# A second step, a product with one, in GpSimd's scaling of attention weights and its minimum

## The chip, the core and the metric

The kernel runs on one core of a Trainium2 chip. A core has five engines that follow their own instruction streams and wait for each other by semaphores: TensorE (PE, with its weight loads PEld), VectorE (DVE), ScalarE (ACT), GpSimd (POOL) and SyncE (SP, which here only issues DMAs). The metric is the device time of one execution in microseconds (us), lower is better.

## The reference

Three layers run one after the other, all in float32: attention with a memory, a gated layer, and a second layer with a squared, cut-off activation.

```python
# attention, B=4, H=8, S=576, D=64
scores = where(causal, -1e9, q @ k.T / 8)
a = exp(scores - scores.max(-1));  a /= a.sum(-1) + 1e-9
local = a @ v
phi = lambda x: where(x > 0, x, exp(x) - 1) + 1
mem = (phi(q) @ M_prev) / ((phi(q) * z_prev).sum(-1) + 1e-6)
x = sigmoid(beta) * mem + (1 - sigmoid(beta)) * local     # -> 2304 x 512
# layer 1 (512 -> 1536 -> 512)
x = (silu(x @ w_gate) * (x @ w_val)) @ w_out
# layer 2 (512 -> 2048 -> 512), g(h) is 0 below -1, h above 1, (h+1)^2/4 between
return g(x @ w_in) @ w_out2
```

The weights `a` are divided by their row sums before the product with v; the kernel does this as a multiplication by one reciprocal per row, and folds the factor 1 - sigmoid(beta) into it.

## The kernel before

The program has two stages, each laid out by its own planner (`Plan`). The first holds the attention and a part of layer 1, the second the rest. This case lives in the first stage, which on the trace fills about the first 260 us.

**The work of the attention.** `Attention.pair(b, n)` describes one pair of heads of one batch entry; there are 16 pairs. For a pair the program loads q, k and v, transposes k and q on TensorE (L607, L618), forms the scores on TensorE (L725 and, for the last 64 rows of both heads together, L759), adds the mask and takes the row extreme on VectorE (L739, L766), and applies exp on ScalarE with the row sums as a by-product (L746, L777). Two small VectorE instructions (L802, L807) then turn the sums into reciprocals `r`, one number for each row. Next comes the scaling of this case (function `scale`, L812 to L820): each tile `a` of attention weights is multiplied in place by its column of `r`. After that TensorE transposes the tile (L830, L852, L869), ScalarE or VectorE copies the transposed tile out of PSUM (L513), and TensorE multiplies with v (L894, L902).

Each pair has nine tiles to scale: four tiles of 128, 256, 384 and 512 columns for each of two heads, since the mask leaves only the lower triangle, and one of 576 columns for the last rows. So the kernel has 144 scalings. A string of digits (`CHOICE`) says for each of them whether GpSimd or VectorE does it: 77 are on GpSimd, 67 on VectorE.

The memory branch works on the same engines: the minimum of q with zero (`f_min`, L635), exp (L638), `p` (L642), its product with z (L647, L651), two folding additions (L658), and the multiplication by the norm (L668). Of the 16 minima one is on GpSimd and 15 on VectorE.

**The early part of layer 1.** TensorE also gets matmuls of layer 1 in this stage (L1308), on the rows of x that are complete.

**What sets the order.** `Plan.order` runs through all tasks by priorities from a fixed list (`RANK`), with a duration for each, and writes each engine's instructions down in the order that results. The engines then follow this order strictly: an instruction that waits holds up all that stand behind it on its engine. The durations that the planner used are formulas in the code. For a scaling on GpSimd it is `c_pool(cols)`, to which the plan adds 43 ns for each task of this engine; for the minimum it is a number written out:

```python
def c_pool(n):                       # L369, ns
    return 0.835 * n + 285
over={"PE": 1, "ACT": 2, "DVE": 9, "POOL": 43},          # L1250
both = [("POOL", c_pool(cols), lambda: f(nc.gpsimd), False),
t = choose("min", [("POOL", 1580, lambda: f_min(nc.gpsimd), False),
```

The change leaves every one of these numbers as it is.

Of the kernel before, what the change touches and what calls it, by code (L numbers as in the profile page):

```python
# [9 lines left out]
F32 = mybir.dt.float32  # L10
# [4 lines left out]
ALU = mybir.AluOpType  # L15
# [4 lines left out]
P = 128  # L20
# [124 lines left out]
class Inst:  # L145


    def __init__(self, tag):
        self.tag, self.left, self.held, self.slot = tag, 0, False, None
# [207 lines left out]
def c_dve(n):  # L357
    return 0.52 * n + 68
# [10 lines left out]
def c_pool(n):  # L369
    return 0.835 * n + 285  # L370
# [23 lines left out]
class Attention:  # L394
# [3 lines left out]
    def __init__(self, ctx, tc, plan, q, k, v, M_prev, z_prev, beta, cst, xs):  # L398
        self.tc, self.nc, self.plan = tc, tc.nc, plan
        nc = tc.nc  # L400
        self.q, self.k, self.v, self.M, self.z, self.beta = q, k, v, M_prev, z_prev, beta
        self.ident = cst["ident"]
        self.xs = xs
        pool = lambda name, bufs: ctx.enter_context(tc.tile_pool(name=name, bufs=bufs))
        self.ld, self.bt, self.ph = pool("ld", 3), pool("bt", 2), pool("ph", 2)
        self.st, self.ap, self.at = pool("st", 3), pool("ap", AB), pool("at", 1)
        self.sm, self.ac = pool("sm", 3), pool("ac", 1)
        self.ps = ctx.enter_context(tc.tile_pool(name="aps", bufs=1, space=PSUM))
        for tags, n in ((("kn", "qn", "vn", "K", "S"), 3), (("zb", "MZ", "a4", "P", "kv", "qz"), 2),
                        (("a0", "a1", "a2", "a3"), AB), (("R1",), RB1),  # L410
                        (("R0_0", "R0_1"), RB0), (("e", "p", "x"), 2), (("mn",), 3), (("bank",), 8)):
            for t in tags:
                plan.cap(t, n)

        ac = self.ac
        self.mask0 = ac.tile([P, 512], F32, name="mask0")
        nc.gpsimd.memset(self.mask0, 0.0)
        nc.gpsimd.affine_select(
            out=self.mask0[:, 384:512], in_=self.mask0[:, 384:512], compare_op=ALU.is_ge,
            fill=MASKED, base=0, pattern=[[-1, P]], channel_multiplier=1)  # L420
        self.mask4 = ac.tile([P, HS], F32, name="mask4")
        nc.gpsimd.memset(self.mask4, 0.0)
        for h in range(2):
            m = self.mask4[h * 64:(h + 1) * 64, HS - 64:HS]
            nc.gpsimd.affine_select(
                out=m, in_=m, compare_op=ALU.is_ge,
                fill=MASKED, base=0, pattern=[[-1, 64]], channel_multiplier=1)

        self.GP = ac.tile([P, NP, 9], F32, name="GP")
        self.OGP = ac.tile([P, NP, 9], F32, name="OGP")  # L430

        self.kn, self.vn = ([ac.tile([P, 4, 2, D], F32, name=f"{x}_{i}") for i in range(3)] for x in ("kn", "vn"))
        self.a4 = [ac.tile([P, 640], F32, name=f"a4_{i}") for i in range(2)]
        self.kv, self.qz, self.MZ = (
            [ac.tile([P, NP, 2, D], F32, name=f"{x}_{i}") for i in range(2)] for x in ("kv", "qz", "MZ"))
        for i in range(2):
            nc.vector.memset(self.kv[i][0:64], 0.0)
            for h in range(2):
                nc.vector.memset(self.qz[i][h * 64:(h + 1) * 64, :, 1 - h], 0.0)
        for i in range(2):  # L440
            nc.gpsimd.memset(self.a4[i][:, S:640], 0.0)
            for h in range(2):
                nc.vector.memset(self.MZ[i][h * 64:(h + 1) * 64, :, 1 - h], 0.0)
# [36 lines left out]
    def pair(self, b, n):  # L480
# [6 lines left out]
        nc, pl = self.nc, self.plan  # L487
        num = b * NP + n
        st = {"a": {}}
# [8 lines left out]
        def choose(name, options, deps=(), uses=()):  # L498
            return pl.choose(None, options, deps, uses)
# [132 lines left out]

        def f_min(eng):
            e = st["e"] = self.ph.tile([P, 9, D], F32, name="e", tag="e")
            eng.tensor_scalar(e, st["qn"], 0.0, None, op0=ALU.min)  # L635

        def f_exp():
            nc.scalar.activation(st["e"], st["e"], AF.Exp)  # L638
# [31 lines left out]
        def tp():  # L670
            p = st["p"]
            t = psum("tp", i_tp)
            for c in range(4):
# [3 lines left out]
            nc.tensor.transpose(t[0:64, 0:128], p[:, 8], self.ident)  # L677

        t = choose("min", [("POOL", 1580, lambda: f_min(nc.gpsimd), False),
                           ("DVE", c_dve(576), lambda: f_min(nc.vector), True)], l_q, [i_q, i_e])  # L680
        t = add("ACT", c_act(576) + 40, "exp", f_exp, [t], [i_e])
        t = add("DVE", c_dve2(576), "phi", f_phi, [t], [i_q, i_e, i_p], True)
# [129 lines left out]
        def scale(key, h, i, cols, name, t_r):  # L812
            def f(eng):
                a = st["a"][key][:, 0:cols]
                o = i if h == 0 else i + 5
                eng.tensor_scalar(a, a, st["mn"]["r"][:, o:o + 1], None, op0=ALU.mult)  # L816

            both = [("POOL", c_pool(cols), lambda: f(nc.gpsimd), False),
                    ("DVE", c_dve(cols) + 60, lambda: f(nc.vector), True)]
            return choose(name + ".sc", both, [t_r], [i_a[key], i_mn])  # L820
# [982 lines left out]
```

## Time and profile before

| | |
|---|---|
| median of 3 runs | 1030.02 us (1028.54 to 1031.4) |
| the profiled execution's own time | 1031.17 us |
| its span on the trace | 1029.4 us |
| PE / PEld busy | 999.6 / 907.3 us |
| DVE / ACT / POOL busy | 681.5 / 623.5 / 154.3 us |
| instructions on POOL | 164 |
| scaling on POOL (L816) | 77 instructions, 96.6 us |

The profiled execution took 1.15 us more than the median, and 1.8 us of it lie outside of the span. All of GpSimd's work stands in the first quarter of the program; afterwards that engine is idle. TensorE's busy figure has to be read with care, since matmuls are pipelined and their ends are modelled: the row of weight loads shows the gaps better. From 300 us on TensorE is almost without a gap.

### The profile page before, as it was taken

Reading aid. Unit: us, or ns where it says so; the run is one execution under the profiler, and the core shown is the slowest. Engines: PE = TensorE matmul, PEld = TensorE weight load, DVE = VectorE, ACT = ScalarE, POOL = GpSimd, SP = SyncE. Lnnn points to the kernel's source line nnn. Section 1 sums busy time; section 2 is a strip of 40 time slices with the busy share of each in tenths; the row PEclk is TensorE's granted clock in tenths of the full one; section 3 lists DMA queues with packets and bytes.
Section 4 is the critical chain, followed back from the end, with each engine's and each line's share of the span. In section 5 each row is a group of like instructions: output and inputs, shape, how many; then the busy total and the mean of one; then the engine's idle time right before and its main releaser. Section 6 shows DMA issues by size and latency. Waiting matters only on the chain.

```text
span 1029.4 us, 16214 instructions
## 1 busy us (share of the span) xinstructions
PE 999.6 (97%) x5898; PEld 907.3 (88%) x5898; DVE 681.5 (66%) x1402; ACT 623.5 (61%) x1221; POOL 154.3 (15%) x164
## 2 busy tenths in 40 slices
PE   6889999999999999999999999999999999999998
PEld 5667767767999999999999999999999988888886
DVE  5799897873697878784657657876654346455541
ACT  3999686874475756655345435566555557666661
POOL 2674777871000000000000000000000000000000
PEclk9999999999999999999999999999999999999999
DMA  7766443221755454453986464266663596324420
GB/s 184 174 164 180 127 116 100 68 68 55 235 170 181 157 175 158 139 200 113 364 294 232 166 202 154 96 222 216 217 224 122 187 363 238 117 83 153 138 93 31
DMA packets 137248, 171.72 MB, mean 167 GB/s; under 512 B 67536, under 2 KB 99280, under 8 KB 137168
## 3 DMA queue, kind: packets, MB, share of 16 engines
q1 hardware_dynamic: 135838, 170.39, 50.6%
q8 instruction: 46, 0.75, 0.3%
q10 hardware_dynamic: 1330, 0.30, 0.2%
q14 instruction: 34, 0.28, 0.1%
HBM read 111.28 MB, written 59.38 MB: 166 GB/s over the span
## 4 chain that ended last, share of the span: by engine, by line
PE 85%; POOL 5%; DVE 3%; DMA 3%; SPq 1%; ACT 1%; issue 1%; ACTq 0%; DVEq 0%; POOLq 0%
PE mm L1531 37%; PE mm L1666 19%; PE mm L1612 15%; POOL a L816 4%; PE av L902 3%; PE s L725 2%; PE mm L1308 2%; PE t L852 2%; DMA xr<-xs 1%; PE av L894 1%; PE s L759 1%; DMA qn<-in_q_dram 1%; PE t L869 1%; DVE a L739 1%; DMA h2s<-r 1%
## 5 line engine op out<-in xcount | busy, mean ns | idle before, releaser
L1531 PE MATMUL mm<-xw 128*128 128x384 f32 x1944 | 347.0, 334 | 1.8 <-ACT r L1557 0.7
L1531 PEld LDWEIGHTS mm<-xw 128*128 128x128 f32 x1944 | 337.7, 188 | 2.9 <-ACT r L1557 1.0
L1666 PE MATMUL mm<-xw 128*128 128x512 f32 x864 | 196.2, 389 | 0.0
L1666 PEld LDWEIGHTS mm<-xw 128*128 128x128 f32 x864 | 162.1, 188 | 33.6
L1612 PE MATMUL mm<-xw 128*128 128x384 f32 x864 | 150.1, 334 | 0.0
L1612 PEld LDWEIGHTS mm<-xw 128*128 128x128 f32 x864 | 149.8, 188 | 0.0
L816 POOL TENSOR_SCALAR a<-a,r 128x128 f32<-128x128 f32 (+4 forms) x77 | 96.6, 1268 | 33.2 <-ACT a L746 15.3
L746 ACT ACTIVATE a<-a,mn 128x256 f32<-128x256 f32 (+3 forms) x128 | 70.8, 556 | 7.5 <-DVE mn L739 6.9
L1655 DVE SCALAR_TENSOR_TENSOR t<-r,t 128x768 f32<-128x768 f32 x48 | 46.0, 958 | 37.5 <-ACT t L1654 36.4
L1434 DVE TENSOR_TENSOR xw<-t,xw 128x768 fp32r<-128x768 f32 x48 | 46.0, 958 | 37.1 <-ACT xw L1431 37.1
L1531 PE MATMUL mm<-xw,wh 128*128 128x384 f32 x324 | 64.8, 334 | 0.0
L1431 ACT CAST xw<-t 128x768 fp32r<-128x768 f32 x48 | 40.1, 834 | 40.6 <-DVE t L1655 40.6
L739 DVE CUSTOM_DVE_ANT_0 a<-s,mask 128x128 f32<-128x128 f32 (+3 forms) x128 | 55.6, 481 | 7.4 <-PE s L725 7.4
L1553 ACT COPY mm<-mm 128x384 f32<-128x384 f32 x54 | 25.1, 465 | 57.4 <-PE mm L1531 57.2
L1531 PEld LDWEIGHTS mm<-xw,wh 128*128 128x128 f32 x324 | 56.9, 188 | 0.0
L513 ACT COPY R<-t 128x384 f32<-128x384 f32 (+2 forms) x97 | 44.7, 501 | 19.8 <-PE t L852 12.6
L1652 ACT ACTIVATE t<-r,half 128x768 f32<-128x768 f32 x48 | 44.9, 936 | 7.3 <-DMA r<-h2s 7.0
L1431 ACT CAST xw<-h 128x768 fp32r<-128x768 f32 x36 | 29.9, 835 | 29.0 <-DMA h<-hs 16.1
L902 PE MATMUL av<-R,vn 128*64 128x320 f32 (+3 forms) x384 | 46.9, 379 | 0.0
L902 PEld LDWEIGHTS av<-R,vn 128*64 128x64 f32 x384 | 27.6, 137 | 20.7
L1434 DVE TENSOR_TENSOR xw<-h,xw 128x768 fp32r<-128x768 f32 x36 | 34.0, 955 | 16.3 <-ACT xw L1431 16.0
L852 PE MATMUL t<-ident,a 128*128 128x128 f32 x224 | 34.3, 277 | 10.0 <-POOL a L816 9.3
(159 smaller groups left out, 1473.9 us busy)
## 6 DMA issues: line engine op xcount, KB each, us to landing
h2s<-r SPq DMA_DIRECT2D x48, 384.0 KB
r<-h2s SPq DMA_DIRECT2D x48, 384.0 KB
raw<-in_moe_w_out_dram SPq DMA_DIRECT2D x28, 512.0 KB
park<-pk SPq DMA_DIRECT2D x28, 512.0 KB
hs<-h SPq DMA_DIRECT2D x33, 384.0 KB
h<-hs SPq DMA_DIRECT2D x33, 384.0 KB
xw<-park SPq DMA_DIRECT2D x24, 512.0 KB
xr<-xs SPq DMA_DIRECT2D x24, 384.0 KB
```

The source lines that it names most:

```text
L739: nc.vector.tensor_tensor_reduce(a, st[f"s{h}{tag}"][:, at_[c]:at_[c] + kl[c]], self.mask0[:, 512 - kl[c]:512], -0.125, 3.0e38, ALU.add, A ...
L746: nc.scalar.activation(a, a, AF.Exp, bias=mn[:, o:o + 1], scale=-1.0, accum_out=sm[:, o:o + 1])
L816: eng.tensor_scalar(a, a, st["mn"]["r"][:, o:o + 1], None, op0=ALU.mult)
L852: nc.tensor.transpose(x[:, kc * P:(kc + 1) * P], a[:, kc * P:(kc + 1) * P], self.ident)
L902: nc.tensor.matmul(o[rg][halves[h], c0:c1], V, r, start=False, stop=i == len(terms[rg]) - 1, tile_position=(0, h * 64), skip_group_check=True)
L1431: nc.scalar.copy(s["x"][:, :, 0], t())
L1434: nc.vector.tensor_sub(s["x"][:, :, 1], t(), f32(s["x"][:, :, 0]))
L1531: nc.tensor.matmul(o, S["k"](k, pw, j), x[k]["at"](px, j), start=begin and not (i or j), stop=j == 1 and i == 2, skip_group_check=True)
L1612: nc.tensor.matmul(o, u["k"](pw, m), h["at"](px, j), start=(p == 0 and j == 0 and n == 0), stop=(p == F1 // 2 - 1 and j == 1 and n == 2), ...
L1652: x1 = add_act(2 * HB, lambda raw=raw, t=t: nc.scalar.activation(t["get"](), raw["get"](), AF.Relu, bias=half, scale=0.5), [x], [raw["i"], ...
L1655: x1 = add_dve(2 * HB, lambda raw=raw, t=t: nc.vector.scalar_tensor_tensor(t["get"](), raw["get"](), 1.0, t["get"](), op0=ALU.max, op1=ALU ...
L1666: nc.tensor.matmul(o, h["at"](px, j)[:, m * P:(m + 1) * P], u["w"][:, pw], start=(i == 0 and j == 0 and n == 0), stop=(i == F2 // 2 - 1 an ...
```

## The change

GpSimd's form of two instructions gets a second arithmetic step. The scaling was a times r; it becomes a times r times `one`, where `one` is a new tile of one column that holds 1.0, so that both factors are read from SBUF, one number for each partition. The minimum was min(q, 0); it becomes min(q, 0) times 1.0, with both operands as constants in the instruction. The values computed are the same. VectorE's forms of both stay as they were. One memset is added at the start, on GpSimd, to fill `one`.

```diff
+        self.one = ac.tile([P, 1], F32, name="one")
+        nc.gpsimd.memset(self.one, 1.0)
...
-            eng.tensor_scalar(e, st["qn"], 0.0, None, op0=ALU.min)
+            if eng is nc.gpsimd:
+                eng.tensor_scalar(e, st["qn"], 0.0, 1.0, op0=ALU.min, op1=ALU.mult)
+            else:
+                eng.tensor_scalar(e, st["qn"], 0.0, None, op0=ALU.min)
...
-                eng.tensor_scalar(a, a, st["mn"]["r"][:, o:o + 1], None, op0=ALU.mult)
+                r = st["mn"]["r"][:, o:o + 1]
+                if eng is nc.gpsimd:
+                    eng.tensor_scalar(a, a, r, self.one, op0=ALU.mult, op1=ALU.mult)
+                else:
+                    eng.tensor_scalar(a, a, r, None, op0=ALU.mult)
```

Every engine's instructions stand in the same order as before, and wait for the same engines. The memset is the one instruction that is added; it stands in GpSimd's first instructions, before the two memsets of the padding of `a4` (L441).

## Rows read from the trace of the kernel before

**Rows 1.** The page, part 1: busy time, share of the span, instructions.
```profile
PE 999.6 (97%) x5898; PEld 907.3 (88%) x5898; DVE 681.5 (66%) x1402; ACT 623.5 (61%) x1221; POOL 154.3 (15%) x164
```
**Rows 2.** Busy time of each engine by stretch: us, engine busy (instructions), clock.
```profile
core 0: us, PE busy (x) PEld busy (x) DVE busy (x) ACT busy (x) POOL busy (x), PEclk, DMA share, GB/s
33.00:245.00 212.00, 196.58 (x1507) 146.52 (x1507) 179.40 (x612) 172.08 (x492) 144.63 (x135) 0.99 0.43 114
...
300.00:1029.00 729.00, 724.87 (x3912) 690.39 (x3912) 450.18 (x678) 407.98 (x645) 0.00 (x0) 1.00 0.51 178
```
**Rows 3.** Chain that ended last, 33 to 262 us: shares, then pieces (start, us).
```profile
by line: POOL a L816 19.1%; PE av L902 14.2%; PE s L725 9.8%; PE mm L1308 9.6%; PE t L852 7.7%; PE av L894 5.8%; PE s L759 3.6%; PE t L869 3.3%; DVE a L739 2.6%; PE tp L674 2.0%; DVE a L816 1.8%; PE t L830 1.7%; DMA xs<-x 1.7%; issue 1.7%; 
...
33.45 6.04 POOL a L816 x5
...
172.95 7.04 POOL a L816 x5
```
**Rows 4.** Line 816: who waited for it (us, times).
```profile
  PEld t L852: 12.0, 10
  PE t L852: 10.0, 8
  PEld t L869: 4.3, 6
  PE t L869: 2.6, 4
...
  PEld t L830: 2.0, 3
  PE t L830: 0.4, 1
```
**Rows 5.** GpSimd's groups by shape: xcount | busy us, mean ns | idle before.
```profile
L816 POOL TENSOR_SCALAR a<-a,r 128x512 f32<-128x512 f32 x18 | 29.1, 1617 | 5.9 <-DVE r L807 2.9 <-ACT a L746 2.6 <-ACT x L914 0.4
L816 POOL TENSOR_SCALAR a<-a,r 128x384 f32<-128x384 f32 x16 | 21.2, 1328 | 11.8 <-ACT a L746 9.3 <-DVE a L816 2.1 <-ACT e L638 0.4
L816 POOL TENSOR_SCALAR a<-a,r 128x256 f32<-128x256 f32 x17 | 17.6, 1037 | 2.4 <-ACT a L746 1.7 <-DVE r L807 0.7
L816 POOL TENSOR_SCALAR a<-a,r 128x576 f32<-128x576 f32 x9 | 16.3, 1811 | 7.7 <-DVE r L807 5.1 <-ACT a L746 1.6 <-PE s L725 1.0
L816 POOL TENSOR_SCALAR a<-a,r 128x128 f32<-128x128 f32 x17 | 13.4, 787 | 5.5 <-DVE r L807 5.5
L647 POOL TENSOR_TENSOR e<-p,zb 128x512 f32<-128x512 f32 x9 | 12.0, 1329 | 5.1 <-DVE p L642 5.1
...
L651 POOL TENSOR_TENSOR e<-p,zh 128x64 f32<-128x64 f32 x9 | 3.1, 341 | 0.0
L1282 POOL CAST xw<-xr 128x768 fp32r<-128x768 f32 x3 | 2.5, 821 | 0.0
L635 POOL TENSOR_SCALAR e<-qn 128x576 f32<-128x576 f32 x1 | 1.7, 1654 | 1.8 <-DVE nrm L655 1.8
...
L465 POOL COPY GP<-gate 128x32 f32<-128x32 f32 x1 | 0.2, 211 | 0.4 <-DVE ogate L460 0.4
...
L1236 POOL MEMSET half<- 128x1 f32 x1 | 0.1, 100 | 0.0
```
**Rows 6.** Three single scalings on GpSimd, in order of time: start, us.
```profile
121.34 0.60 POOL L816 TENSOR_SCALAR a<-a,r 128x128 f32<-128x128 f32 x1
...
177.04 1.24 POOL L816 TENSOR_SCALAR a<-a,r 128x384 f32<-128x384 f32 x1
...
178.26 1.72 POOL L816 TENSOR_SCALAR a<-a,r 128x576 f32<-128x576 f32 x1
```
**Rows 7.** TensorE's weight loads and VectorE, 33 to 262 us: other waits (us, times, longest).
```profile
PEld tp L674 <- DVE p L668: 2.8, 2, 2.0
PEld av L894 <- DVE mn L739: 2.4, 5, 0.8
PEld av L894 <- ACT a L746: 1.7, 3, 0.8
```

## The prediction

> **What bounds the kernel now.** I read the page first. TensorE is busy for 97% of the span, GpSimd for 15% [rows 1], which would make GpSimd look harmless. The busy time by stretch corrects that. All of the scaling lies between 33 and 245 us, and there GpSimd is busy for 144.6 of 212 us, VectorE for 179.4, ScalarE for 172.1; TensorE's weight loads, whose gaps are the more honest sign of a waiting TensorE, for only 146.5, so that 65.5 us of that stretch are without a load. From 300 us on TensorE has work for 724.9 of 729 us and GpSimd has none [rows 2]. So nothing behind the attention can become shorter by this change, and what the attention gains or loses is handed on whole: the second stage only starts earlier or later.
>
> The chain of waits says what ends last in the attention. From 33 to 262 us its largest item is GpSimd's scaling with 19.1%, which of 229 us is 43.7 us; the chain goes through queues of two to seven scalings in a row, such as five in 6.04 us and five in 7.04 us [rows 3]. The view of line 816 says who pays: TensorE's weight loads waited for it 12.0 + 4.3 + 2.0 = 18.3 us, its matmuls 10.0 + 2.6 + 0.4 = 13.0 us [rows 4]. A scaling on GpSimd is thus on the path, at least in part, and the question is what its new form costs.
>
> **What a scaling costs today.** Single undisturbed ones took 0.60 us for 128 columns, 1.24 for 384, 1.72 for 576 [rows 6]. That is a straight line: (1.72 - 0.60) us / 448 columns = 2.5 ns a column, and 0.60 - 128 x 2.5 ns = 0.28 us fixed. The groups' means stand higher, 787 ns at 128 columns and 1811 at 576 [rows 5], since some of the 77 ran beside VectorE's work and were held up. The columns over all 77 are 18 x 512 + 16 x 384 + 17 x 256 + 9 x 576 + 17 x 128 = 27,072 [rows 5]; at 2.5 ns these are 67.7 us of the 96.6.
>
> 2.5 ns a column is dear for one product. The cast of 768 columns took 821 ns and the copy of 32 took 211: (821 - 211) / 736 = 0.83 ns a column. The product of two streamed tensors took 1329 ns at 512 columns and 341 at 64, (1329 - 341) / 448 = 2.2 ns a column, and it fetches twice as much as a scaling [rows 5]. So neither fetching the data nor multiplying explains the 2.5 ns; the one-step form of this instruction itself has a slow way through the columns, one third as fast as a copy.
>
> **The change part by part.**
> The memset of `one` is a 128x1 memset; the one of `half` took 100 ns [rows 5]. It stands among the first instructions, 30 us ahead of the first scaling. Cost nothing; without that cover 0.1 us.
>
> The minimum on GpSimd is one instruction of 1654 ns [rows 5]. At the copy's rate 0.96 us would go, at worst one more pass of 2.5 ns for each of 576 columns would add 1.4 us. A single instruction, well ahead of its users: I take nothing for it.
>
> The second factor is one more number for each partition to be fetched. No row shows a form with two. The nearest is the difference between a scaling of 576 columns with one such number, 1.72 us, and the minimum of as many with none, 1.65 us [rows 5, 6]: 0.07 us. For 77 scalings that is 5.4 us of GpSimd's time; below, nothing.
>
> The second step's price for each column is the unknown. No row shows a GpSimd instruction of this kind with two steps. From below the bound is the copy's 0.83 ns: it reads and writes each column once, as any form must, so 1.67 ns a column would be saved, 45.2 us over 27,072 columns. From above, the second step could cost as much as the first, 2.5 ns more, 67.7 us. I take the lower end. Two reasons: a scaling is slower than a product of two tensors with twice the reading, so its loop does something besides the work, and an instruction whose second step is filled in is the complete form, for which a straight loop is the natural one. And the planner's own formula for a scaling, 0.835 n + 285 ns, has the fixed part of today's scalings (0.28 us), while a copy's is 211 - 32 x 0.83 = 184 ns; but its slope is the copy's. Whoever wrote it had, as I read it, timed an instruction of this kind that went through the columns at 0.83 ns. That is an inference from code and no measurement, and for the minimum the planner has 1580, close to the slow 1654 of the trace.
>
> The Trainium skill has a rule that speaks against the change (GPSIMD Engine Reference, section 3.1): a loop body with one or two operations per element is bound by the port at about 1.03 cycles an element, so a second operation would neither cost nor give anything. The rows disagree for the one-step form with their 2.5 ns, three times that. If the two-step form alone followed the rule, the page's figure would put it near my lower end; if the number of steps truly did not matter, the result would be the no-change rival below.
>
> Now the sum. On GpSimd 45.2 - 5.4 = 39.8 us go, of 96.6. Of the 96.6 us, 43.7 lie on the chain [rows 3], 45%, so 18.0 us leave the chain if nothing else is late. Something will be: the weight loads also wait for VectorE's norm product (2.8 us), the row extremes (2.4 us) and ScalarE's exp (1.7 us) [rows 7], and these are what a transposed tile or a product with v meets next. The other way to count is by what TensorE lost to the scaling: 18.3 us by its loads, 13.0 by its matmuls [rows 4]; a wait that is shorter than the time saved in the queue before it goes wholly, and most are, with 0.96 us on average (18.3 / 19) against some 2.9 us saved in a queue of five (5 x 27,072 / 77 columns x 1.67 ns). Between 13 and 18 I take 15 us. GpSimd then waits more itself, for ScalarE's exp and the reciprocals, as it did already for 9.3 us ahead of the 384-column tiles and 5.5 ahead of the 128-column ones [rows 5]; that costs nothing. Shorter scalings also block VectorE less where the two collide; I count nothing for it.
>
> The profiled execution took 1031.17 us, 1.15 above the median of 1030.02. 1031.17 - 15 = 1016.2, and against the median 1015 us.
>
> **The rivals.**
> No change. The loop stays as slow, or becomes as fast as the product of two tensors at 2.2 ns. Then between nothing and 0.3 x 27,072 = 8.1 us are saved and up to 5.4 us are added, times 45%: from -3.6 to +2.4 us, about 1030 (1026 to 1033). For it: the trace shows no instruction of this kind on GpSimd that is fast, the minimum included. Against it: 2.5 ns for one product is slower than two reads, and something must be behind that.
>
> Also near here: GpSimd becomes fast, but the planned order holds the gain back, because VectorE (179.4 of 212 us) and ScalarE (172.1) take over as what is late [rows 2]. Both have 33 us and 40 us of idle time in the stretch, so 15 us fit; if only a third of the chain's gain came through it would be 6 us, 1024. This is within the forecast's own range.
>
> Slower. Each step is a pass of its own in the loop. If the second costs one copy's visit, 0.83 ns a column, 22.5 + 5.4 = 27.9 us are added on GpSimd; 45% is 12.6 us on the chain, 1042 us. If it costs as much as the first, 67.7 + 5.4 = 73.1 us, GpSimd would have 144.6 + 73.1 = 217.7 us of work in a stretch of 212 and set the pace itself: 45% is 33 us, 1063 us. It decides as soon as the second step costs anything that the fetch of `one` does not hide; the place is the queue of scalings ahead of the transposes. For it: more arithmetic for each column on an engine that is already slow there. Against it: at 2.5 ns the arithmetic can't be the limit if a cast goes through at 0.83.
>
> **How the numbers follow.** The forecast has 0.80, no change 0.10, slower 0.10. About 0.3%, 3 us, is what a measurement of this kernel can tell from no change. The forecast's own range reaches from 1003 us, if the saving of the chain is exceeded because freed waits let other queues close up as well, to 1024 us, if a third comes through. The range for 8 in 10 is 1003 to 1027: it leaves out the slower case and nearly all of the no-change case. Faster by over 0.3%: 0.80 and a third of the no-change case, 0.83. Within: 0.07. Slower: 0.10.
>
> **What would show it.** In the profile after, GpSimd's scalings should take about 0.4 us at 128 columns and 0.8 at 576, in place of 0.60 and 1.72; their group should fall from 96.6 to some 55 us. TensorE's loads should wait for line 816's successor for under 5 us in place of 18.3, its share of the chain should be less than half, and the end of the attention's last product should come some 15 us earlier, with the second stage as long as before. If the rate per column is 2.2 ns or more, the forecast's cause is wrong. If the rate falls as said and the time moves by less than 6 us, the step from GpSimd's busy time to the chain is wrong.

## The result, and the profile after

The changed kernel took 1013.22 us in the median of 4 runs (1012.69 to 1013.86), the kernel before on the same chip 1030.63 us; the ratio is 0.9834, with a 95% interval of 0.9817 to 0.9852. That is 17.4 us less. The span of the profiled execution went from 1029.4 to 1012.1 us, 17.3 us less.

GpSimd's groups by shape in the profile after, to be held against [rows 5] (line 823 is the scaling with two steps, line 638 the minimum with two):

```profile
L823 POOL TENSOR_SCALAR a<-a,r,one 128x512 f32<-128x512 f32 x18 | 15.2, 846 | 8.2 <-DVE r L812 4.5 <-ACT a L751 3.0 <-ACT x L923 0.7
...
L823 POOL TENSOR_SCALAR a<-a,r,one 128x576 f32<-128x576 f32 x9 | 8.7, 964 | 9.3 <-DVE r L812 5.9 <-ACT a L751 2.0 <-PE s L730 1.4
...
L638 POOL TENSOR_SCALAR e<-qn 128x576 f32<-128x576 f32 x1 | 2.1, 2145 | 1.1 <-DVE nrm L660 1.1
```

The mean of a 512-column scaling fell from 1617 to 846 ns and that of a 576-column one from 1811 to 964. The minimum went the other way, from 1654 to 2145 ns: a second step does not make an instruction faster by itself. Single undisturbed scalings, in order of time, answer to [rows 6]:

```profile
72.02 0.45 POOL L823 TENSOR_SCALAR a<-a,r,one 128x128 f32<-128x128 f32 x1
...
152.85 0.82 POOL L823 TENSOR_SCALAR a<-a,r,one 128x576 f32<-128x576 f32 x1
...
153.66 0.77 POOL L823 TENSOR_SCALAR a<-a,r,one 128x512 f32<-128x512 f32 x1
```

(0.82 - 0.45) us / 448 columns = 0.83 ns a column, in place of 2.5, and 0.45 - 128 x 0.83 ns = 0.34 us fixed, in place of 0.28. Who waited for the scaling on GpSimd, in the view of its line (us, times):

```profile
  PEld t L878: 0.8, 1
  PEld t L839: 0.5, 1
  PEld t L861: 0.5, 2
```

These three rows are all of them, 1.8 us. The rows before that answer to them are not quite those of [rows 4]: there both engines' scalings stood on line 816, and VectorE's are counted with GpSimd's. The lists of waits by engine take them apart, the weight loads' first and the matmuls' second (33 to 262 us of the kernel before; us, times, longest):

```profile
PEld t L830 <- POOL a L816: 1.3, 2, 0.7
```

```profile
PE t L852 <- POOL a L816: 9.3, 7, 2.1
```

With these two rows, and the others as in [rows 4], GpSimd alone kept the weight loads waiting for 12.0 + 4.3 + 1.3 = 17.6 us before, and the matmuls for 9.3 + 2.6 = 11.9 us.

The chain from 33 to 262 us no longer lists GpSimd among its largest items, where it stood first with 19.1% [rows 3]; TensorE's matmuls have taken its place:

```profile
by line: PE av L911 17.7%; PE s L730 13.5%; PE mm L1317 11.3%; PE t L861 10.1%; PE av L903 7.2%; PE s L764 5.6%; PE t L878 4.3%; ACT a L751 3.9%; DMA xr<-xs 3.9%; PE t L839 3.0%; PE tp L679 2.5%; PE tk L609 2.2%; PE tq L620 2.0%; DMA xs<-x 
```

Busy time by stretch, as in [rows 2]:

```profile
33.00:245.00 212.00, 208.86 (x1627) 159.66 (x1628) 177.71 (x613) 174.69 (x499) 106.35 (x135) 1.00 0.47 122
```

In the same 212 us TensorE now starts 1627 matmuls where it had 1507. The start of the last product of attention weights with v tells where the saving lies; the row of that line gives min, median and max of a duration, then the first and the last start. Before:

```profile
L902 PE MATMUL av<-R,vn x384: 272/406/433, 44.0 to 257.9; 128*64 128x320 f32 x96, 128*64 128x192 f32 x32, 128*64 128x256 f32 x32, 128*64 128x128 f32 x32
```

And after:

```profile
L911 PE MATMUL av<-R,vn x384: 272/406/483, 41.5 to 241.1; 128*64 128x320 f32 x96, 128*64 128x192 f32 x32, 128*64 128x256 f32 x32, 128*64 128x128 f32 x32
```

From 257.9 to 241.1 us are 16.8 of the 17.3 us; the rest of the program starts that much earlier and is as long as it was, to within 0.5 us.

### The profile page after: what moved, and what is told of

Same layout as the page of the kernel before. It is cut to its first block, busy times and chain, and to the rows that moved or that the text cites. A ratio compares the mean times of both kernels' runs of the same rounds, so it can differ in the third digit from the quotient of the medians.

```text
span 1012.1 us, 16215 instructions
## 1 busy us (share of the span) xinstructions
PE 995.0 (98%) x5898; PEld 907.0 (90%) x5898; DVE 678.4 (67%) x1402; ACT 621.4 (61%) x1221; POOL 116.8 (12%) x165
## 4 chain that ended last, share of the span: by engine, by line
PE 92%; DMA 3%; ACT 2%; DVE 1%; SPq 1%; issue 0%; ACTq 0%; DVEq 0%
PE mm L1540 38%; PE mm L1675 19%; PE mm L1621 15%; PE av L911 4%; PE s L730 3%; PE mm L1317 3%; PE t L861 2%; PE av L903 2%; PE s L764 2%; DMA xr<-xs 1%; PE t L878 1%; ACT a L751 1%; DMA qn<-in_q_dram 1%; PE t L839 1%; PE tk L609 1%; PE tq L620 1%
## 5 line engine op out<-in xcount | busy, mean ns | idle before, releaser
L823 POOL TENSOR_SCALAR a<-a,r,one 128x128 f32<-128x128 f32 (+4 forms) x77 | 57.9, 763 | 44.0 <-DVE r L812 22.5
L1443 DVE TENSOR_TENSOR xw<-h,xw 128x768 fp32r<-128x768 f32 x36 | 34.0, 954 | 14.9 <-ACT xw L1440 14.7
L1047 DVE TENSOR_TENSOR xw<-wp,xw 128x768 fp32r<-128x768 f32 x36 | 34.0, 954 | 12.1 <-ACT xw L1045 12.0
```

The lines of the kernel that those rows point to most:

```text
L823: eng.tensor_scalar(a, a, r, self.one, op0=ALU.mult, op1=ALU.mult)
L1443: nc.vector.tensor_sub(s["x"][:, :, 1], t(), f32(s["x"][:, :, 0]))
```

## The experiments

Three questions stood open: what it is in the new form that makes it fast; whether the path takes a fixed share of what GpSimd's work changes, as the prediction's sum has it; and whether anything is left to gain there. Each kernel below is the changed one with one edit, the last one with three; where an edit reads `self.zero`, that is a tile of one column filled with 0.0, made as `one` is. The times are to be held against the kernel before on the same chip: 1030.65 us for the constant, the addition, the maximum as the second step and the one-step minimum; 1029.48 us for the two kernels with both forms and the one with one column; 1030.8 us for the minimum from tiles, the maximum as the first step and the try for a better kernel.

**What makes it fast.** First the factor one as a constant in the instruction:

```diff
-                    eng.tensor_scalar(a, a, r, self.one, op0=ALU.mult, op1=ALU.mult)
+                    eng.tensor_scalar(a, a, r, 1.0, op0=ALU.mult, op1=ALU.mult)
```

> The scaling keeps two steps, a product with r and a product with one, but the 1.0 is a constant in the instruction and not a tile. In the profile of the change the two-step minimum, with two constants, took 2145 ns at 576 columns where the one-step form had 1654, while the two-step scaling, with two tiles, fell to 0.83 ns a column. Theory A (the fast loop belongs to the pair product, product, wherever the second factor is kept): 0.83 ns a column, about 0.39 us at 128 columns and 0.75 to 0.83 at 576, time 1012 to 1014 us. Theory B (the fast loop needs both factors in tiles): as slow as the minimum or worse, 1.9 to 2.2 us at 576 columns, time 1030 to 1045 us.

It took 1013.43 us, ratio 0.9825 (0.9795 to 0.9854). Two single scalings of it, in order of time:

```profile
36.08 0.37 POOL L823 TENSOR_SCALAR a<-a,r 128x128 f32<-128x128 f32 x1
...
155.01 0.69 POOL L823 TENSOR_SCALAR a<-a,r 128x512 f32<-128x512 f32 x1
```

(0.69 - 0.37) / 384 is 0.83 ns a column again, and each is 0.08 us shorter than with the tile (0.45 and 0.77 us above): theory B is refuted. The tile `one` isn't needed. Its 77 fetches take time on GpSimd (the group took 50.4 us, and 57.9 with the tile) but don't show in the kernel's time.

Next the second operation, an addition of zero and then a maximum with zero, both from a tile:

```diff
-                    eng.tensor_scalar(a, a, r, self.one, op0=ALU.mult, op1=ALU.mult)
+                    eng.tensor_scalar(a, a, r, self.zero, op0=ALU.mult, op1=ALU.add)   # first kernel
+                    eng.tensor_scalar(a, a, r, self.zero, op0=ALU.mult, op1=ALU.max)   # second kernel
```

> The second step is an addition of zero from a tile, in place of the product with one. Theory A (the fast loop belongs to the pair product, product): slow, 2.5 to 3.4 ns a column, time 1030 to 1042 us. Theory B (two filled steps with both factors in tiles, whatever the operations): 0.83 ns a column, time 1012 to 1015 us. A third one, that products and additions have a fast loop and comparisons none, expects the same as B here.

> The second step is the maximum with zero from a tile, in place of the product with one (the weights are not negative). Theory B (two filled steps with both factors in tiles, whatever the operations): 0.83 ns a column, time 1012 to 1015 us. Theory A (product, product alone) and the third (products and additions alone): slow, about 3.3 ns a column as the minimum of the change had ((2145 - 340) / 576 is 3.1), 1.9 to 2.2 us at 576 columns. Then GpSimd's scaling grows from 96.6 us in the kernel before by 0.6 to 0.8 ns for each of 27,072 columns, 16 to 22 us, and with 45% of it on the chain the time is 1037 to 1041 us: the slower rival of the prediction, made on purpose.

The addition took 1013.44 us, ratio 0.9826 (0.9798 to 0.9855), with 0.82 us for 576 columns:

```profile
152.32 0.82 POOL L825 TENSOR_SCALAR a<-a,r,zero 128x576 f32<-128x576 f32 x1
```

The maximum took 1056.17 us, ratio 1.0239 (1.0210 to 1.0268). Two single scalings of the kernel with the maximum, in order of time:

```profile
193.24 0.79 POOL L825 TENSOR_SCALAR a<-a,r,zero 128x128 f32<-128x128 f32 x1
...
198.06 2.28 POOL L825 TENSOR_SCALAR a<-a,r,zero 128x576 f32<-128x576 f32 x1
```

(2.28 - 0.79) / 448 = 3.33 ns a column, against 2.5 for one step and 0.83 for two products. So theory A is too narrow (an addition will do) and B is wrong: the operations decide. On the slow way the second step costs another 0.83 ns a column, which is the price that the prediction's slower rival put on it. The rate came out as expected and the time did not: with 45% of GpSimd's extra work on the path I had expected 1037 to 1041 us, and it took 15 us more than that. Two more kernels, with one run each, ask where the comparison and the numbers have to stand. The minimum with its two numbers in tiles:

```diff
-                eng.tensor_scalar(e, st["qn"], 0.0, 1.0, op0=ALU.min, op1=ALU.mult)
+                eng.tensor_scalar(e, st["qn"], self.zero, self.one, op0=ALU.min, op1=ALU.mult)
```

> The two-step minimum with zero and one read from tiles, in place of constants; everything else as in the change. Rule O (only the operations decide: products and additions have the fast loop, a comparison has not): as slow as with constants, 2.15 us plus about 0.08 us for each number fetched, 2.2 to 2.35 us. Rule F (where the factors are kept decides for a comparison): 0.82 us. The kernel's time is that of the change either way, 1012 to 1015 us.

And the scaling with the maximum as the first step:

```diff
-                    eng.tensor_scalar(a, a, r, self.one, op0=ALU.mult, op1=ALU.mult)
+                    eng.tensor_scalar(a, a, self.zero, r, op0=ALU.max, op1=ALU.mult)
```

> The maximum with zero as the first step and the product with r as the second; both numbers from tiles. Rule O (any comparison among the two steps takes the slow loop): 3.3 ns a column, 2.28 us at 576 columns, and 1053 to 1059 us, as when the maximum stood second. Rival (the second step alone chooses the loop, a product there is enough): 0.82 us at 576 columns and 1012 to 1015 us; the minimum of the change, with a product second at 2.15 us, speaks against it, but with constants.

The minimum from tiles took 2286 ns (1012.62 us in all), the scaling with the maximum first 2.28 us at 576 columns (1055.6 us). The first row is the minimum's group, the second a single scaling:

```profile
L640 POOL TENSOR_SCALAR e<-qn,zero,one 128x576 f32<-128x576 f32 x1 | 2.3, 2286 | 1.1 <-DVE nrm L662 1.1
```

```profile
197.28 2.28 POOL L825 TENSOR_SCALAR a<-a,zero,r 128x576 f32<-128x576 f32 x1
```

Rule O holds in both: a comparison in either place takes the slow way, and a product as the second step does not rescue it. Not tested are a single addition, a single product with a constant, other operations and other types than float32; why the slow forms are slow stays open.

**The minimum by itself.** The scaling as in the change, the minimum with one step:

```diff
-                eng.tensor_scalar(e, st["qn"], 0.0, 1.0, op0=ALU.min, op1=ALU.mult)
+                eng.tensor_scalar(e, st["qn"], 0.0, None, op0=ALU.min)
```

> The scaling as in the change, the minimum with one step as before. The two-step minimum took 0.49 us more in the profile of the change and nobody waited for it. Theory: no part of the gain comes from the minimum; the time is that of the change, 1012.5 to 1014 us, and the minimum takes 1.65 us. Rival: the longer minimum holds up the queue behind it, and 0.5 us more are gained, 1012 to 1013 us; a measurement can hardly tell these two apart, but a difference of over 3 us either way would refute both.

It took 1014.49 us, ratio 0.9831 (0.9798 to 0.9864), the minimum 1662 ns. That is 0.5 us above the expected range, and its own runs go from 1013.13 to 1014.97 us. The gain is the scaling's; the minimum's half a microsecond can't be seen either way.

**How GpSimd's time becomes the kernel's.** Two kernels use the two-step form for a part of the scalings only, once for the first two batch entries and once for the first head of each pair with the shared tile:

```diff
-                    eng.tensor_scalar(a, a, r, self.one, op0=ALU.mult, op1=ALU.mult)
+                    eng.tensor_scalar(a, a, r, self.one if b < 2 else None, op0=ALU.mult, **({"op1": ALU.mult} if b < 2 else {}))
...
+                    eng.tensor_scalar(a, a, r, self.one if h == 0 else None, op0=ALU.mult, **({"op1": ALU.mult} if h == 0 else {}))
```

> The two-step form only for the scalings of the first two batch entries: 32 of the 77 on GpSimd, 11,392 of 27,072 columns; the other 45 have one step. Theory K (each stretch of the attention gives up its own stall, and what a stretch gives is handed on whole): the gain is about the share of the chain's GpSimd pieces that lies in the first half, 16 of 43.7 us, 6 to 8 us of the 17.4, so 1022.5 to 1025 us; weight loads still wait for the one-step scalings, those behind about 130 us, for some 8 to 10 us. Rival R (what is gained early is lost to the later, still slow stretch, since its queues only wait longer): 1027 us or more.

> The two-step form only for the scalings of the first head of each pair and of the shared tile of 576 columns: 43 of 77, 16,192 of 27,072 columns, spread over all of the attention. Rule P of the prediction (the path takes a fixed share, 45%, of what GpSimd's work changes): the gain goes by columns, 60% of 17.4 us, so 1020 us (1019 to 1021.5). Theory K (a stall is what the queue exceeds the other engines' slack by; the first part of a shortening is worth more than the last, and a lengthening counts nearly whole, as the 30.8 us added with the maximum cost 25.5): over 75% of the gain, 1013.5 to 1017.5 us.

The first took 1023.4 us, ratio 0.9931 (0.9908 to 0.9954): 6.1 us gained, as expected, so an early gain isn't eaten by a stretch that stays slow. Most of those who waited for its scalings on GpSimd (us, times; its one-step scalings start at 137.9 us):

```profile
  PEld t L861: 5.7, 4
  PE t L861: 4.5, 4
  PEld t L878: 3.6, 5
  PE t L878: 2.0, 3
```

The second took 1019.24 us, ratio 0.9896 (0.9875 to 0.9917): 10.2 us, which is what the fixed share gives and not the 75% of the gain that I expected from theory K. The last kernel of this kind leaves almost all of the scaling's work out; only the first column of each tile is scaled:

```diff
-                    eng.tensor_scalar(a, a, r, self.one, op0=ALU.mult, op1=ALU.mult)
+                    eng.tensor_scalar(a[:, 0:1], a[:, 0:1], r, self.one, op0=ALU.mult, op1=ALU.mult)
```

> The scaling on GpSimd touches only the first column of each tile; the other columns of these 77 tiles stay unscaled. This shows what is left to gain on GpSimd. The group falls from 57.9 us to 77 x about 0.35 us, 27 us and less. Theory K (with the change GpSimd's scaling is off the path: weight loads waited for it 1.8 us in all): 1009.5 to 1013.5 us. Rule P: 45% of the 31 us go, 14 us, and the time is 999 us.

It took 1014.02 us, ratio 0.9848 (0.9821 to 0.9875), 0.5 us above what theory K had and 15 us above rule P: another 24 us less on GpSimd brought nothing. Weight loads waited for it 1.8 us, as in the change. Its group:

```profile
L823 POOL TENSOR_SCALAR a<-a,r,one 128x1 f32<-128x1 f32 x77 | 33.8, 454 | 55.5 <-DVE r L812 28.5 <-ACT a L751 17.0 <-PE av L911 3.9
```

It is GpSimd that waits now, 55.5 us, for the reciprocals, ScalarE's exp and TensorE.

Put in a row by the scaling's busy time on GpSimd, with the start of the last product with v:

| kernel | scaling on GpSimd, us | last product starts, us | us on the path for each us on GpSimd, from the row above |
|---|---|---|---|
| product, then maximum | 126.6 | 284.5 | |
| before | 96.6 | 257.9 | 26.6 / 30.0 = 0.89 |
| two steps in the first two batch entries | 56.1 + 24.4 = 80.5 | 251.4 | 6.5 / 16.1 = 0.40 |
| two steps for the first head | 42.1 + 31.5 = 73.6 | 246.0 | 5.4 / 6.9 = 0.78 |
| after | 57.9 | 241.1 | 4.9 / 15.7 = 0.31 |
| one column only | 33.8 | 242.0 | nothing |

Each start is read from one execution. The kernel with two steps in the first two batch entries ran from 1020.77 to 1026.21 us, and the profiled execution was its slowest; so the ratios 0.40, 0.78 and 0.31 of the middle rows can't be told apart, and the two middle kernels differ besides in which scalings were shortened. By the medians of the time, each against the kernel before on its chip, 6.1 / 16.1 = 0.38, 10.2 / 23.0 = 0.44 and 17.4 / 38.7 = 0.45 of what GpSimd lost left the time.

Neither K nor P fits the whole table. From 96.6 down to 57.9 us the share of rule P holds, and K's larger worth of the first part isn't seen. Below 57.9 us P fails and K holds: the share is zero. Above 96.6 us 25.5 / 30.0 = 0.85 of the added work showed in the time, which speaks for K, but TensorE's clock fell there too (last section), so this isn't settled.

**A try for a better kernel.** The constant 1.0, the one-step minimum, and the 21 scalings of 512 and 576 columns that VectorE had moved to GpSimd:

```diff
+            if cols >= 512:
+                self.plan.chosen += 1
+                return add("POOL", c_pool(cols), name + ".sc", lambda: f(nc.gpsimd), [t_r], [i_a[key], i_mn])
             return choose(name + ".sc", both, [t_r], [i_a[key], i_mn])
```

> A try for a better kernel: the 21 scalings of 512 and 576 columns that VectorE had go to GpSimd too, with the product with a constant 1.0 (0.69 and 0.75 us each) and the one-step minimum; the planner makes a new order from this. GpSimd gets about 15 us more, VectorE some 10 us less. Theory (TensorE holds the path in the attention, 92% of the whole chain, and neither VectorE nor GpSimd): no gain, 1011 to 1018 us. Rival (VectorE, 178 of 212 us busy, still holds the order up): 1003 to 1009 us.

It took 1022.86 us, ratio 0.9921 (0.9891 to 0.9951), 4.9 us above the upper end of what the theory expected, and some 9 above the change. Both the theory and its rival missed. GpSimd is not the reason, since weight loads waited for it 1.6 us in all. The longest wait of the weight loads for another engine in its attention (33 to 262 us; us, times, longest) is for a scaling on VectorE:

```profile
PEld t L864 <- DVE a L825: 4.2, 1, 4.2
```

The last product with v starts at 249.2 us. The mean granted clock from 33 to 245 us was 0.98 here and 1.00 in the change, which can be worth up to 0.02 x 212 us = 4.2 us. The planner made another order, with other waits, and how the 9 us divide among them and the clock isn't shown. It does not beat the change.

## Why the prediction was right

**Where the kernel is bound.** As said: the scaling lay on the path, the second stage kept its length, and the saving appears whole between 33 and 241 us.

**The price for each column.** Right: 0.83 ns, the lower end. The reason given for it was only half right. "An instruction whose second step is filled in is the complete form" is refuted: filled with a maximum it costs 3.33 ns, and the filled minimum got slower. What decides is the pair of operations: product and product, or product and addition, went the fast way. That the second step tried here was a product and not a maximum was, as far as this reason goes, luck. The reading of the planner's formula, that its author had timed something at 0.83 ns with the scaling's fixed part, agrees with the numbers, which do not show what was timed: with the constant 1.0 the fixed part is 0.37 us - 128 x 0.83 ns = 0.26 us, and the formula has 0.285.

**The second factor.** 0.07 us forecast, 0.34 - 0.28 = 0.06 measured, 0.08 when taken away by itself. GpSimd's group lost 96.6 - 57.9 = 38.7 us, where 39.8 were forecast.

**The memset and the minimum.** Nothing, as taken. The minimum's bound from above, 1.4 us more, held with 0.49 us more.

**From GpSimd to the path.** This term came out on the good side: 15 us forecast between 13 and 18, 16.8 measured. Two readings under it were not quite right, without changing the sum: the waits of [rows 4] hold VectorE's scalings too (GpSimd's alone are 17.6 and 11.9 us), and the queues of scalings on the chain are of two to five, not seven. The three waits that were named as late next were there afterwards, hardly longer, in the same list of the weight loads' waits as [rows 7] (whole kernel after; us, times, longest):

```profile
PEld av L903 <- DVE mn L744: 2.8, 5, 0.8
PEld tp L679 <- DVE p L673: 2.1, 1, 2.1
...
PEld av L903 <- ACT a L751: 1.7, 3, 0.8
```

That speaks for a discount smaller than 3 us, but there is another candidate, for which the prediction has no term: TensorE's clock. Its two levels are 1.2 and 2.4 GHz, and a granted clock of 1.00 is the upper one. In the kernel before it fell once between 33 and 245 us, after the weight loads had waited 2.4 us for a scaling, their longest such wait. First the stretch, then two pieces of the chain (start, us):

```profile
150.00:165.00 15.00, 11.68 (x72) 10.44 (x69) 9.82 (x37) 8.66 (x25) 12.38 (x12) 0.89 0.36 92
```

```profile
159.78 1.92 PE mm L1308 x6
...
164.17 1.06 PE mm L1308 x6
```

Six matmuls of layer 1 took 1.92 us on the chain, and the next six 1.06 us. A mean of 0.89 is 3.3 of 15 us at the lower level, which can have cost half of that at most, some 1.6 us. After the change the clock from 33 to 245 us was 1.00. So the 1.8 us above the forecast can be the discount, the clock or both; no run separates them.

The 45% as a fixed share held for the steps between the kernel before and the change. It comes from one execution's chain and is no law: by it the 24 us of the one-column kernel would have been worth some 11 us, and they were worth nothing; the 27.9 us of the slower rival were priced at 12.6 us, and the kernel with the maximum, with 30.0 us more on GpSimd, cost 25.5, of which an unknown part is TensorE's clock.

**The number of steps.** The Trainium skill (GPSIMD Engine Reference, section 3.1) has a body of one or two operations per element bound by the port at about 1.03 cycles an element. The trace does not agree with one rate for both: one product took 2.5 ns a column, two products 0.83 ns, and a product with a maximum 3.33 ns. The number of operations alone does not tell the rate here.

## What to carry to other kernels

Take the cost of an instruction form from single undisturbed instances at two sizes and compare its slope with that of a copy on the same engine; a slope of three times the copy's for one product is a reason to try an equivalent form. Forms with the same result differed here by a factor of three (one product against two) and four (the maximum against the product with one). An engine with a low share of the span can still hold the path of one stage, so read its busy time by stretch and who waited for it, with the granted clock of the same stretch beside it. And once nobody waits for it, stop: the next 24 us that GpSimd lost were worth nothing.

## What the runs showed that I had not expected

A second step that multiplies by one makes GpSimd's scaling, a product written as `tensor_scalar` in float32, three times faster for each column (2.5 to 0.83 ns), adding zero does the same, and a maximum in either step makes it slower (3.33 ns).

The kernel with the maximum also lost clock. Busy time and clock of three stretches of that kernel:

```profile
160.00:175.00 15.00, 10.26 (x62) 8.14 (x61) 10.56 (x39) 8.89 (x26) 13.44 (x11) 0.85 0.46 119
175.00:190.00 15.00, 14.84 (x93) 11.59 (x94) 9.08 (x33) 8.96 (x26) 10.25 (x10) 0.81 0.19 48
...
200.00:215.00 15.00, 11.88 (x77) 10.36 (x75) 9.60 (x29) 7.67 (x21) 13.09 (x13) 0.77 0.27 79
```

A mean of 0.77 to 0.85 between the levels of 1.2 and 2.4 GHz means that TensorE ran at half speed for 30% to 46% of these stretches. In the first two its weight loads waited for GpSimd's scaling, 2.9 and 2.8 us in all; in the third for a product on VectorE, 3.6 us. Over the whole attention (33 to 288 us) these waits are:

```profile
PEld t L863 <- POOL a L825: 24.6, 14, 3.9
...
PEld tp L681 <- DVE p L675: 5.6, 2, 3.6
```

The mean over 33 to 245 us was 0.94 there, 0.99 before [rows 2] and 1.00 after. So a part of the 25.5 us is probably TensorE's lower clock and not the wait itself, by these means at most (0.99 - 0.94) x 212 us = 10.6 us. How large it is, no run shows; without it the added work could have counted for as little as 14.9 / 30.0 = 0.50, close to the share of rule P.
